# Retention and MLP on one core: first loads on other queues, another order of loads and blocks, and casts one burst later

## The chip, the core and the metric

The kernel runs on one core of a Trainium2 chip. The core has five engines with instruction streams of their own: TensorE (PE, matmuls), VectorE (DVE), ScalarE (ACT), GpSimd (POOL) and SyncE (SP). SP, ACT and POOL can issue DMA transfers. The metric is the device time of one execution, in microseconds (us); lower is better.

## The reference, cut to what matters

```python
# q, k, v: (8, 8, 576, 64) f32: batch, heads, positions, head width
scores = (1 / sqrt(64)) * q @ k.T                    # per batch and head
gamma  = 1 - 2 ** (-5 - arange(8))                   # one per head
Dmat   = where(i >= j, gamma ** (i - j), 0)          # i, j: positions
x = ((scores * Dmat) @ v) -> (4608, 512)             # tokens x (heads * width)
h = x @ w_in                                         # w_in:  (512, 2048)
g = maximum(0.01 * h, h)
out = g @ w_out                                      # w_out: (2048, 512), out f32
```

The first part is retention: attention with a decay in place of the softmax. It can be computed in chunks, with a running state per head that is carried from chunk to chunk. The second part is an MLP with a leaky activation.

## The kernel before, in words

**Units and groups.** The 4608 tokens are cut into 36 units of 128 tokens (two chunks of 64). Four units make a group of 512 tokens; there are nine groups. A batch has nine chunks, so in some units (4, 13 and so on) the second chunk begins a new batch. The three loads of such a unit are split into two DMAs each.

**What a unit goes through.** `load` brings k, q and v of the unit (256 KB each) into three buffers, six of each kind. `cast_k` (ACT, L172) turns k into f16; `cast_q` (L175) and `cast_v` (L179) multiply by a decay table and turn into f16, on DVE for units 0 to 7 and on POOL later. q and k are then transposed: on PE for units 0 to 7 (`transpose_pe`, L200, with a copy out of PSUM at L207; `turn` is both), by a DMA on SP for later ones (`transpose_dma`, L183). `scores` (L215, L224) computes q times k and each chunk's contribution to the state; `masks` (L233) applies the causal mask; `state` (L255 to L261) adds to the running state and `state_cast` (L273, L276) makes the f16 copy of it. `outputs` (L291, L302) or `outputs_acc` (L321, L333) computes the unit's x. With `outputs`, two steps bring x into the f16 tile xT: `own` (ACT, L355) and `add` (DVE, L360). With `outputs_acc` one copy does (`x_copy`, ACT, L341).

**The MLP.** The first product (`h_mm`, L373) works on blocks of w_in columns, with the leaky step behind each on ACT (L387). `h_half` takes two column blocks and 256 tokens, `h_unit` four blocks and the 128 tokens of one unit, `h_block` one block and 512 tokens. Their PSUM tiles and those of the transposes come from one pool of four. w_in is loaded in four quarters of two DMAs each by POOL, with a cast to f16; the pairs of blocks 0 and 1 of `halves` use quarter 0, 2 and 3 quarter 1, 4 and 5 quarter 2, 6 and 7 quarter 3. The second product is plain for group 0 (`wide`, L423). From group 1 on it is a scheme of seven half-size products (`seven`, L483) on sums of g (`mix`) and of w_out (`mix_weights`). In `seven` the first product is copied out by ACT (`keep`, L495, the tile k1) before PE may go on adding to the same PSUM tile.

**What sets the order.** The order on each engine is the order of the calls, written out by hand (`manual_schedule`). Each engine runs its instructions in that order, and waits where an operand isn't ready. Some names:

- `burst(u)`: scores of u, outputs of u - 1, masks, state and state cast (POOL) of u, own and add of u - 1.
- `ahead(u)`: cast of k on ACT, of q and v on POOL, and the DMA transpose on SP.
- `step(u)`, in the steady part: `burst(u)`, `load(u + 4)`, `ahead(u + 2)`.
- `early(u)`, L758: the form of `step` for units 9 to 12. `early(9)` is called in the wide products, `early(10)` between them and `seven(1, ...)`, `early(11)` and `early(12)` by hooks after the first and the fifth product of `seven(1, ...)`.
- `keep_warm(n)`: products of zeros into an unused tile.
- `settle`, `finish`, `finish2`: state and masks of a unit; its outputs and what brings them to xT.

In the first 50 us the order is a long list by hand (L560 to L756): POOL issues most loads, SP a few, and units 0 to 7 run between the blocks of groups 0 and 1.

Of the kernel before, what the change touches and what calls it, by code (L numbers as in the profile page):

```python
# [18 lines left out]
def kernel(  # L19
# [9 lines left out]
    nc = tc.nc  # L29
# [54 lines left out]
    def behind(dma, *others):  # L84
        for o in others:
            tc.add_manual_dep(
                dma.ins,
                o.ins.name,
                mybir.DependencyInfo(
                    mybir.DependencyClass.Sync, mybir.DependencyReason.DATA  # L90
                ),
                reason="order of loads",
            )
# [17 lines left out]
    last_load = {}  # L111
    carry = [None]

    def half(i):
        return slice(CH * i, CH * i + CH)
# [3 lines left out]
    def load(u, eng=None, after=None):  # L119
        for x in (1, 0, 2):  # L120
            t = ld_pool.tile([P, H, D], FP, name=f"t32_{x}")
            t32[u, x] = t
            c = 2 * u
            same = c % CB + 1 < CB
            e = eng[x] if isinstance(eng, dict) else eng or nc.sync
            engs = e if isinstance(e, tuple) else (e,)
            n = H // len(engs)
            for j, rows in ((0, P),) if same else ((0, CH), (1, CH)):
                b, w = (c + j) // CB, (c + j) % CB
                for i, e in enumerate(engs):  # L130
                    hs = slice(n * i, n * i + n)
                    d = e.dma_start(  # L132
                        out=t[CH * j : CH * j + rows, hs],
                        in_=(q, k, v)[x][b, hs, CH * w : CH * w + rows, :].rearrange(
                            "h t d -> t h d"
                        ),
                    )
                    if after is not None and (x in after or not isinstance(after, dict)):
                        behind(d, *(after[x] if isinstance(after, dict) else after))
                        after = None  # L140
                    last_load[u, x] = d
# [3 lines left out]
    def load_w_in(f, after=None):  # L145
        fs = slice(f * FQ, (f + 1) * FQ)
        rows = moe_w_in.rearrange("(o c k) f -> o k c f", o=2, k=CH)
        ds = []
        for o in range(2):
            ds.append(nc.gpsimd.dma_start(out=w_in16[half(o), :, fs], in_=rows[o][:, :, fs]))  # L150
            if after is not None and not o:
                behind(ds[0], *after)
        return ds
# [20 lines left out]
    def cast_q(u, eng):  # L174
        eng.tensor_tensor(out=qk16[u][:, 0], in0=t32[u, 0], in1=decay(u, 0), op=MUL)  # L175
# [91 lines left out]
    def live(u, j):  # L267
        return (2 * u + j) % CB != CB - 1

    def state_cast(u, copy, js=(0, 1)):  # L270
        js = [j for j in js if live(u, j)]
        if len(js) == 2:
            copy(out=st16[u], in_=s32s[u])  # L273
        else:
            for j in js:
                copy(out=st16[u][:, j], in_=s32s[u][:, j])  # L276
# [94 lines left out]
    def h_mm(hps, n, g, f, ts):  # L371
        for c in range(NP):
            nc.tensor.matmul(  # L373
                out=hps[:, n, :],
                lhsT=w_in16[:, c, f * P : (f + 1) * P],
                rhs=xT[g][:, c, ts],
                start=(c == 0),
                stop=(c == NP - 1),
            )

    def g_tile(g):
        if g not in g_t:
            g_t[g] = g_pool.tile([P, NF, TOK], F16, name="gt")
        return g_t[g]

    def leaky(out, in_):
        nc.scalar.activation(out=out, in_=in_, func=mybir.ActivationFunctionType.Lrelu)  # L387
# [13 lines left out]
    def h_unit(u, fb):  # L401
        g, t0 = u // 4, (u % 4) * P
        ts = slice(t0, t0 + P)
        hps = acc_pool.tile([P, 4, P], FP, name="acc")
        for n in range(4):
            h_mm(hps, n, g, 4 * fb + n, ts)
        leaky(g_tile(g)[:, 4 * fb : 4 * fb + 4, ts], hps)
# [140 lines left out]
    def keep_warm(n):  # L548
        t = acc_pool.tile([P, 1, TOK], FP, name="acc")
        for _ in range(n):  # L550
            nc.tensor.matmul(out=t[:, 0, :], lhsT=idle[:, 0:P], rhs=idle, start=True, stop=True)
# [6 lines left out]
    pool_copy, act_copy, dve_copy = nc.gpsimd.tensor_copy, nc.scalar.copy, nc.vector.tensor_copy  # L558

    keep_warm(7)  # L560
    load(0, {1: nc.sync, 0: (nc.sync, nc.gpsimd), 2: nc.gpsimd})
    load(1, {1: nc.sync, 0: nc.gpsimd, 2: nc.gpsimd})
    load(2, nc.gpsimd)
    load(3, {1: nc.sync, 0: nc.gpsimd, 2: nc.gpsimd}, {1: (last_load[1, 1],)})
    load_w_in(0)
    load_w_in(1)
    load_w_in(2)
    load(4, nc.gpsimd)
    load_w_in(3)
    for u in range(5, 8):  # L570
        load(u, nc.gpsimd)
    w_out_loads = [d for n in range(4) for d in load_w_out(n)]


# [10 lines left out]
    for u in range(4):  # L585
        n = u + 1
        scores(u)
        if not u:
            keep_warm(3)
        state(u, 0)  # L590
        state_cast(u, dve_copy, (0,))
        masks(u)
        if not u:
            cast_q(1, nc.vector)
            cast_v(1, nc.vector)
        state(u, 1)
        if n < 4:
            transpose_pe(n, 1)
            transposed(n, 1, act_copy)
            if not u:  # L600
                keep_warm(3)
                outputs_acc(0)
                x_copy(0)
                keep_warm(1)
            transpose_pe(n, 0)
            transposed(n, 0, act_copy)
            keep_warm(3 if u else 2)
        if n < 3:
            cast_k(n + 1)
            cast_q(n + 1, nc.vector)  # L610
            cast_v(n + 1, nc.vector)
        state_cast(u, act_copy, (1,))
        if u == 1:
            outputs_acc(1)
            x_copy(1)
            keep_warm(2)
        elif u == 2:
            outputs_acc(2)
            x_copy(2)


    def halves(g, *items):
        for a, fb in items:
            h_half(g, a, fb)

    def cast_qv(u):
        cast_q(u, nc.vector)
        cast_v(u, nc.vector)

    def turn(u, x):  # L630
        transpose_pe(u, x)
        transposed(u, x, dve_copy)
# [7 lines left out]
    def finish(u):  # L640
        outputs_acc(u)
        x_copy(u)
        state_cast(u, act_copy, (1,))

    def finish2(u):
        outputs(u)
        own(u)
        add(u)
# [6 lines left out]
    def burst(u, out=True):  # L655

        if u < NU:
            scores(u)
        if out:
            outputs(u - 1)  # L660
        if u < NU:
            masks(u)
            state(u, 0)
            state(u, 1)
            state_cast(u, pool_copy)
        if out:
            own(u - 1)
            add(u - 1)

    def ahead(u):  # L670

        if u >= NU:
            return
        cast_k(u)
        cast_q(u, nc.gpsimd)
        cast_v(u, nc.gpsimd)
        transpose_dma(u)
# [10 lines left out]

    halves(0, (0, 0), (0, 1))
    finish2(3)  # L690
    halves(0, (0, 2), (0, 3), (1, 0))
    cast_k(4)
    cast_qv(4)
    halves(0, (1, 1), (1, 2))
    turn(4, 1)
    halves(0, (1, 3))
    turn(4, 0)
    halves(0, (0, 4))
    scores(4)
    settle(4)  # L700
    halves(0, (0, 5), (1, 4))
    finish2(4)
    state_cast(4, act_copy, (1,))
    halves(0, (1, 5))
    cast_k(5)
    cast_qv(5)
    halves(0, (0, 6), (0, 7))
    turn(5, 1)
    halves(0, (1, 6))
    turn(5, 0)  # L710
    halves(0, (1, 7))
    scores(5)
    settle(5)
    cast_k(6)
    cast_qv(6)
    h_unit(4, 0)
    turn(6, 1)
    cast_k(7)
    h_unit(4, 1)
    finish(5)  # L720
    turn(6, 0)
    h_unit(5, 0)
    scores(6)
    settle(6)
    cast_qv(7)
    h_unit(5, 1)
    turn(7, 1)
    halves(1, (0, 4))
# [2 lines left out]
    halves(1, (0, 5))  # L731
    scores(7)
    settle(7)
    halves(1, (0, 6), (0, 7))
    load(8, after=(w_out_loads[2],))
    load(9)
    h_unit(6, 0)
    finish(7)
    h_unit(6, 1)
# [4 lines left out]
    mix_weights(1, 0)  # L744
    mix_weights(1, 1)
    halves(1, (1, 4))
    ahead(8)
    load(10)
    mix_weights(2, 0)
    mix_weights(2, 1)  # L750
    halves(1, (1, 5), (1, 6))
    ahead(9)
    load(11)
    mix_weights(3, 0)
    mix_weights(3, 1)
    halves(1, (1, 7))  # L756

    def early(u, out=True):  # L758
        burst(u, out)
        if 8 < u < 12:  # L760
            ahead(u + 3)
            load(u + 5)

    at = {
        0: lambda: mixes(1, 0),
# [1 line left out]
        3: lambda: mixes(1, 1),  # L767
        4: lambda: (burst(8, False), ahead(11), load(13)),
        7: lambda: mixes(1, 2),
        9: lambda: early(9),  # L770
    }
    for n in range(16):
        wide(n // 4, n % 4)
        if n in at:
            at[n]()
    early(10)
    seven(1, {0: [lambda: early(11)], 4: [lambda: early(12)]})

    first = [f for i in range(4) for f in (i, i + HF)]
    second = [f for i in range(4, 8) for f in (i, i + HF)]  # L780
# [46 lines left out]
```

## Time and profile before

| | |
|---|---|
| six runs, median | 295.99 us |
| six runs, lowest and highest | 293.57 and 296.88 us |
| the profiled execution | 296.88 us, of it 295.1 us of span |
| mean granted TensorE clock | 0.992 |
| PE busy | 284.0 us, 96% of the span |
| DVE, ACT, POOL busy | 58%, 49%, 35% |
| DMA | 50.01 MB, mean 169 GB/s |

The span is the time from the first to the last instruction of the profiled execution. Busy shares are averages over the whole span: stages with different limits lie behind them. In the lines of the timeline the first number is the start in us and the second the length. In square brackets stands how long the engine had been idle before, and what ended that wait. In tables of windows there follow, for each stretch, the busy us (and number of instructions) of PE, PE's weight loads, DVE, ACT and POOL, then the granted clock, the busy share of the DMA engines (over 1 where queues overlap) and GB/s.

### The profile page before, as it was taken

What the parts mean: (1) busy time and instruction counts of PE and PEld (TensorE: products, weight loads), DVE (VectorE), ACT (ScalarE), POOL (GpSimd) and SP (SyncE); (2) the same over time, 40 slices, a digit from 0 to 9 for tenths busy, and PEclk for the clock granted to TensorE, in tenths of its full rate; (3) what the DMA queues carried; (4) which work ended last, traced back from release to release, by engine and by line L of the source; (5) the groups of instructions that cost most, each with busy time, mean ns of one, the idle gap of its engine ahead of it and who ended that gap; (6) DMA issues with size and microseconds to landing.
All of it is one profiled execution on the core that took longest, in us unless ns stands there. A gap on an engine that the chain in (4) does not pass through costs nothing.

```text
span 295.1 us, 9446 instructions
## 1 busy us (share of the span) xinstructions
PE 284.0 (96%) x4118; PEld 193.1 (65%) x4118; DVE 170.0 (58%) x293; ACT 143.8 (49%) x254; POOL 103.7 (35%) x124
## 2 busy tenths in 40 slices
PE   7898999999699999999999999999999999999994
PEld 3567887745585478547854785478448844884583
DVE  1874478954543477357736763577358546740342
ACT  3657765623224761476157515751674166306610
POOL 8859602536340333333424342334225414000000
PEclk9999999999899999999999999999999999999999
DMA  7999999499999996986599767979995251002003
GB/s 219 274 235 202 294 197 194 105 244 177 185 235 218 285 207 156 256 191 157 131 227 223 175 142 203 217 93 179 246 216 133 50 178 38 4 37 108 0 2 142
DMA packets 132218, 50.01 MB, mean 169 GB/s; under 512 B 121776, under 2 KB 126512, under 8 KB 132176
## 3 DMA queue, kind: packets, MB, share of 16 engines
q1 hardware_dynamic: 125904, 39.73, 59.9%
q0 software_dynamic: 5984, 9.57, 14.6%
q8 instruction: 32, 0.52, 0.7%
q10 hardware_dynamic: 288, 0.11, 0.1%
q14 instruction: 10, 0.08, 0.1%
HBM read 36.81 MB, written 9.44 MB: 157 GB/s over the span
## 4 chain that ended last, share of the span: by engine, by line
PE 87%; DMA 3%; DVE 3%; POOL 2%; SPq 2%; ACT 1%; issue 1%; DVEq 0%; POOLq 0%
PE acc L373 41%; PE acc L483 34%; PE acc L423 4%; PE sc L215 3%; DMA t<-in_v_dram 2%; POOL t L132 2%; PE sc L224 1%; PE ot L291 1%; PE ot L302 1%; SPq L132 1%; DMA t<-in_q_dram 1%; PE ot L321 1%; PE acc L200 1%; DVE s L233 1%; SPq L183 1%
## 5 line engine op out<-in xcount | busy, mean ns | idle before, releaser
L373 PE MATMUL acc<-xT,w_in 128*128 128x512 f16 (+2 forms) x768 | 130.9, 326 | 1.2 <-DVE xT L360 0.8
L387 ACT ACTIVATE gt<-acc 128x512 f16<-128x512 f32 x144 | 85.8, 598 | 57.5 <-PE acc L373 55.7
L373 PEld LDWEIGHTS <-w_in 128*128 128x128 f16 x768 | 68.2, 98 | 52.7 <-issue 1.5
L483 PEld LDWEIGHTS <-gt 128*128 128x128 f16 x640 | 62.0, 98 | 11.3 <-issue 2.0
L233 DVE TENSOR_TENSOR s<-sc,cs 128x512 f16<-128x512 f32 x36 | 24.7, 686 | 41.6 <-PE sc L224 39.5
L483 PE MATMUL acc<-w_out,gt 128*128 128x256 f16 x384 | 46.3, 274 | 2.3 <-ACT k L495 2.1
L273 POOL CAST st<-s 128x512 f16<-128x512 f32 x21 | 12.8, 611 | 81.9 <-DVE s L257 53.7
L175 POOL TENSOR_TENSOR qk<-t,cs 128x512 f16<-128x512 f32 x28 | 29.9, 1069 | 31.5 <-DMA t<-in_q_dram 28.6
L355 ACT COPY own<-ot 128x512 f32<-128x512 f32 x30 | 17.6, 586 | 36.5 <-PE ot L302 29.2
L179 POOL TENSOR_TENSOR v<-t,cs 128x512 f16<-128x512 f32 x28 | 31.4, 1122 | 2.3 <-DMA t<-in_v_dram 1.4
L172 ACT CAST qk<-t 128x512 f16<-128x512 f32 x36 | 22.3, 619 | 20.2 <-DMA t<-in_k_dram 13.2
L483 PE MATMUL acc<-w_mix,mix 128*128 128x256 f16 x256 | 30.8, 280 | 0.0
L467 DVE TENSOR_TENSOR mix<-gt 128x1024 f16<-128x1024 f16 x16 | 14.1, 880 | 29.0 <-ACT gt L387 29.0
L483 PE MATMUL acc<-w_mix,gt 128*128 128x256 f16 x256 | 30.6, 273 | 0.0
L483 PEld LDWEIGHTS <-mix 128*128 128x128 f16 x256 | 25.7, 101 | 3.8 <-DVE mix L467 0.2
L360 DVE TENSOR_TENSOR xT<-ot,own 128x512 f16<-128x512 f32 x30 | 20.5, 683 | 4.6 <-ACT own L355 4.6
L257 DVE TENSOR_TENSOR s<-sc,s 128x256 f32<-128x256 f32 x40 | 16.8, 419 | 3.2 <-PE sc L224 2.7
L508 DVE TENSOR_TENSOR osb<-acc,u 128x512 f32<-128x512 f32 (+1 forms) x17 | 11.1, 656 | 8.0 <-PE acc L483 8.0
L215 PEld LDWEIGHTS <-qkT 64*64 64x64 f16 x576 | 7.7, 107 | 11.3 <-issue 10.4
L423 PE MATMUL acc<-w_out,gt 128*128 128x512 f16 x64 | 14.3, 379 | 0.0
L276 POOL CAST st<-s 128x256 f16<-128x256 f32 x7 | 3.2, 456 | 31.3 <-DVE s L261 17.3
L467 DVE TENSOR_TENSOR mix<-mix,gt 128x1024 f16<-128x1024 f16 x16 | 13.1, 827 | 0.5
(52 smaller groups left out, 240.9 us busy)
## 6 DMA issues: line engine op xcount, KB each, us to landing
out_dram<-osb SPq DMA_DIRECT2D x17, 512.0 KB, 3.7
t<-in_k_dram SPq DMA_DIRECT2D x28, 256.0 KB, 3.7
t<-in_q_dram SPq DMA_DIRECT2D x25, 256.0 KB, 4.2
t<-in_v_dram SPq DMA_DIRECT2D x25, 256.0 KB, 4.9
w_in<-in_moe_w_in_dram POOLq DMA_DIRECT2D x8, 256.0 KB, 7.9
w_out<-in_moe_w_out_dram POOLq DMA_DIRECT2D x4, 512.0 KB, 10.4
t<-in_v_dram POOLq DMA_DIRECT2D x7, 256.0 KB, 5.7
t<-in_q_dram POOLq DMA_DIRECT2D x6, 256.0 KB, 5.9
```

The costliest lines, as they stand in the source:

```text
L172: nc.scalar.copy(out=qk16[u][:, 1], in_=t32[u, 1])
L175: eng.tensor_tensor(out=qk16[u][:, 0], in0=t32[u, 0], in1=decay(u, 0), op=MUL)
L179: eng.tensor_tensor(out=v16[u], in0=t32[u, 2], in1=decay(u, 1), op=MUL)
L233: nc.vector.tensor_tensor(out=s16s[u], in0=sc_tiles[u][:, :, 0], in1=mask_sb.unsqueeze(1).unsqueeze(1).to_broadcast([P, 2, NP, CH]), op=MUL,)
L257: nc.vector.tensor_tensor(out=to, in0=st, in1=carry[0], op=ADD)
L355: nc.scalar.copy(out=owns[u], in_=ot_tiles[u][:, :, 0:NP].rearrange("q j c t -> q c j t"))
L360: nc.vector.tensor_tensor(out=x_of(u).rearrange("q (c g) t -> q c g t", g=2), in0=ot_tiles[u][:, :, NP : 2 * NP].rearrange("q g (c j) t -> ...
L373: nc.tensor.matmul(out=hps[:, n, :], lhsT=w_in16[:, c, f * P : (f + 1) * P], rhs=xT[g][:, c, ts], start=(c == 0), stop=(c == NP - 1),)
L387: nc.scalar.activation(out=out, in_=in_, func=mybir.ActivationFunctionType.Lrelu)
L423: nc.tensor.matmul(out=ys[tb], lhsT=g_t[0][:, f, tb * P : (tb + 1) * P], rhs=w_out16[:, f, :], start=(f == 0), stop=(f == NF - 1),)
L467: nc.vector.tensor_tensor(out=z[:, fs], in0=a[:, fs], in1=b[:, fs], op=op)
L483: nc.tensor.matmul(out=r[name][:, tb, :], lhsT=lhs[:, f, tb * P : (tb + 1) * P], rhs=rhs[:, f, :], start=fresh and n == 0, stop=f == HF - ...
```

## The change

- **First loads.** The second half of q of unit 0 (heads 4 to 7) is issued by ACT instead of POOL; the first half stays on SP. k of unit 3 is issued by POOL instead of SP, without the dependency on k of unit 1.
- **Order on POOL.** The loads of unit 4 are issued ahead of quarter 2 of w_in, and those of unit 5 ahead of quarter 3, where before they stood after quarter 2 and after quarter 3.
- **State cast of unit 3.** Its second part moves from before the first two half blocks to after `finish2(3)`.
- **Blocks.** In groups 0 and 1 the half blocks, the two unit blocks of unit 4, the turns and the casts of unit 7's q and v are put in another order. The number of blocks stays the same.
- **Loads 8 to 11.** Loads 8 and 9 are called ahead of two half blocks, loads 10 and 11 ahead of `ahead(8)` and `ahead(9)` instead of behind them.
- **Casts.** `ahead(13)` and `load(15)` move from after `burst(10)` to after `burst(11)`, `ahead(14)` and `load(16)` from after `burst(11)` to after `burst(12)`.

```diff
--- before.py
+++ after.py
@@ -558,17 +558,18 @@
     pool_copy, act_copy, dve_copy = nc.gpsimd.tensor_copy, nc.scalar.copy, nc.vector.tensor_copy
 
     keep_warm(7)
-    load(0, {1: nc.sync, 0: (nc.sync, nc.gpsimd), 2: nc.gpsimd})
+    load(0, {1: nc.sync, 0: (nc.sync, nc.scalar), 2: nc.gpsimd})
     load(1, {1: nc.sync, 0: nc.gpsimd, 2: nc.gpsimd})
     load(2, nc.gpsimd)
-    load(3, {1: nc.sync, 0: nc.gpsimd, 2: nc.gpsimd}, {1: (last_load[1, 1],)})
+    load(3, nc.gpsimd)
     load_w_in(0)
     load_w_in(1)
+    load(4, nc.gpsimd)
     load_w_in(2)
-    load(4, nc.gpsimd)
+    load(5, nc.gpsimd)
     load_w_in(3)
-    for u in range(5, 8):
-        load(u, nc.gpsimd)
+    load(6, nc.gpsimd)
+    load(7, nc.gpsimd)
     w_out_loads = [d for n in range(4) for d in load_w_out(n)]
 
 
@@ -609,7 +610,8 @@
             cast_k(n + 1)
             cast_q(n + 1, nc.vector)
             cast_v(n + 1, nc.vector)
-        state_cast(u, act_copy, (1,))
+        if u < 3:
+            state_cast(u, act_copy, (1,))
         if u == 1:
             outputs_acc(1)
             x_copy(1)
@@ -688,41 +690,42 @@
 
     halves(0, (0, 0), (0, 1))
     finish2(3)
+    state_cast(3, act_copy, (1,))
     halves(0, (0, 2), (0, 3), (1, 0))
     cast_k(4)
     cast_qv(4)
-    halves(0, (1, 1), (1, 2))
+    halves(0, (1, 1))
     turn(4, 1)
+    halves(0, (1, 2))
+    turn(4, 0)
     halves(0, (1, 3))
-    turn(4, 0)
-    halves(0, (0, 4))
     scores(4)
     settle(4)
-    halves(0, (0, 5), (1, 4))
+    halves(0, (0, 4), (0, 5))
     finish2(4)
     state_cast(4, act_copy, (1,))
-    halves(0, (1, 5))
     cast_k(5)
     cast_qv(5)
-    halves(0, (0, 6), (0, 7))
+    halves(0, (1, 4), (1, 5))
     turn(5, 1)
-    halves(0, (1, 6))
+    h_unit(4, 0)
     turn(5, 0)
-    halves(0, (1, 7))
+    h_unit(4, 1)
     scores(5)
     settle(5)
     cast_k(6)
     cast_qv(6)
-    h_unit(4, 0)
+    halves(0, (0, 6), (0, 7))
+    finish(5)
+    halves(0, (1, 6))
     turn(6, 1)
     cast_k(7)
-    h_unit(4, 1)
-    finish(5)
+    halves(0, (1, 7))
     turn(6, 0)
+    cast_qv(7)
     h_unit(5, 0)
     scores(6)
     settle(6)
-    cast_qv(7)
     h_unit(5, 1)
     turn(7, 1)
     halves(1, (0, 4))
@@ -731,9 +734,9 @@
     halves(1, (0, 5))
     scores(7)
     settle(7)
-    halves(1, (0, 6), (0, 7))
     load(8, after=(w_out_loads[2],))
     load(9)
+    halves(1, (0, 6), (0, 7))
     h_unit(6, 0)
     finish(7)
     h_unit(6, 1)
@@ -744,22 +747,21 @@
     mix_weights(1, 0)
     mix_weights(1, 1)
     halves(1, (1, 4))
+    load(10)
     ahead(8)
-    load(10)
     mix_weights(2, 0)
     mix_weights(2, 1)
     halves(1, (1, 5), (1, 6))
+    load(11)
     ahead(9)
-    load(11)
     mix_weights(3, 0)
     mix_weights(3, 1)
     halves(1, (1, 7))
 
-    def early(u, out=True):
-        burst(u, out)
-        if 8 < u < 12:
-            ahead(u + 3)
-            load(u + 5)
+    def early(u, n):
+        burst(u)
+        ahead(n)
+        load(n + 2)
 
     at = {
         0: lambda: mixes(1, 0),
@@ -767,14 +769,14 @@
         3: lambda: mixes(1, 1),
         4: lambda: (burst(8, False), ahead(11), load(13)),
         7: lambda: mixes(1, 2),
-        9: lambda: early(9),
+        9: lambda: early(9, 12),
     }
     for n in range(16):
         wide(n // 4, n % 4)
         if n in at:
             at[n]()
-    early(10)
-    seven(1, {0: [lambda: early(11)], 4: [lambda: early(12)]})
+    burst(10)
+    seven(1, {0: [lambda: early(11, 13)], 4: [lambda: early(12, 14)]})
 
     first = [f for i in range(4) for f in (i, i + HF)]
     second = [f for i in range(4, 8) for f in (i, i + HF)]
```

## The prediction

> **What bounds the kernel now.** I read the page's busy shares first, then the matmul engine's waits, then the chain of waits, then the timeline around each hole, and last the windows of one microsecond.
>
> The page says that the matmul engine is nearly always busy, so the end moves only by closing its holes, by raising its clock, or by letting useful matmuls start sooner.
>
> ```profile
> PE 284.0 (96%) x4118; PEld 193.1 (65%) x4118; DVE 170.0 (58%) x293; ACT 143.8 (49%) x254; POOL 103.7 (35%) x124
> ```
>
> The waits of that engine name the holes (engine, line, releaser, us in total, times, longest):
>
> ```profile
> PE acc L483 <- ACT k L495: 2.1, 1, 2.1
> ...
> PE acc L373 <- DVE xT L360: 0.8, 1, 0.8
> PE acc L200 <- DVE v L179: 0.6, 1, 0.6
> ...
> PE acc L373 <- ACT xT L341: 0.3, 1, 0.3
> ```
>
> The timeline shows the largest: the cast of unit 13's k (L172) sits on ScalarE ahead of the copy k1 (L495) and waits 3.04 us for its load; the matmul waits for the copy.
>
> ```profile
> 76.33 0.62 ACT L172 CAST qk<-t 128x512 f16<-128x512 f32 x1 [3.04 <-DMA t<-in_k_dram]
> 76.85 0.58 ACT L495 COPY k<-acc 128x512 f32<-128x512 f32 x1
> 77.48 2.34 PE L483 MATMUL acc<-w_out,gt 128*128 128x256 f16 x16 [2.06 <-ACT k L495]
> ```
>
> The chain (start, us, what) gives a second price: these 64 products take 8.81 us behind the hole, and the same 64 one group later 7.15. The windows say why: the granted clock (the figure after the five engines) is 0.50 for three microseconds.
>
> ```profile
> 77.48 8.81 PE acc L483 x64
> ...
> 108.32 7.15 PE acc L483 x64
> ```
> ```profile
> 79.00:80.00 1.00, 1.00 (x6) 0.74 (x5) 0.00 (x0) 0.00 (x0) 0.20 (x1) 0.50 1.00 363
> 80.00:81.00 1.00, 1.00 (x7) 0.71 (x5) 0.00 (x0) 0.00 (x0) 0.44 (x1) 0.50 2.60 140
> 81.00:82.00 1.00, 1.00 (x7) 0.69 (x6) 0.00 (x0) 0.00 (x0) 1.00 (x2) 0.50 0.98 57
> ```
>
> Before 24 us the engine is filled with dummy products; there the first data and VectorE set the pace. VectorE waits 4.54 us for q of unit 0, then 0.92 for v; at 23.03 it adds only after ScalarE's copy, which stood behind the state cast (1.88 idle).
>
> ```profile
> 1.27 0.94 POOL L132 DMA_DIRECT2D t<-in_q_dram  x1 [0.82 <-POOLq L811]
> 2.21 0.92 POOL L132 DMA_DIRECT2D t<-in_v_dram  x1
> 5.83 0.69 DVE L175 TENSOR_TENSOR qk<-t,cs 128x512 f16<-128x512 f32 x1 [4.54 <-DMA t<-in_q_dram]
> 7.44 0.69 DVE L179 TENSOR_TENSOR v<-t,cs 128x512 f16<-128x512 f32 x1 [0.92 <-DMA t<-in_v_dram]
> 21.13 0.41 ACT L276 CAST st<-s 128x256 f16<-128x256 f32 x1 [1.88 <-DVE s L261]
> 23.03 0.69 DVE L360 TENSOR_TENSOR xT<-ot,own 128x512 f16<-128x512 f32 x1 [1.93 <-ACT own L355]
> 23.77 2.78 PE L373 MATMUL acc<-xT,w_in 128*128 128x256 f16 x24 [0.81 <-DVE xT L360]
> ```
>
> **The base of the sum.** The profiled execution took 296.88 us: 295.1 of span and 1.8 around it. It is the slowest of six; the median, 295.99, is 0.9 lower, the lowest 3.3 lower. The sum is made against 296.88.
>
> **First unit.** GpSimd's first issue goes: every later one up to v of unit 2 comes one issue, 0.9 us, earlier. k of unit 3 moves from SP to GpSimd and takes the freed place, so q and v of unit 3 and all w_in issues keep their times. ScalarE gains one issue (0.57 us by SP's row for the same half). It falls ahead of the table load at 1.64, and the cast of k at 3.69 has 0.56 idle before it: +0.05, and k's path is not the last. When does q land? The rows of this size: 4.0 us from SP, 4.5 from GpSimd. From an issue at about 1.65 that is 5.6 to 6.1, with another ring in the contest; against that, nothing stands ahead of it on its ring but two constants. I take 5.5 against 5.77 before: -0.3; bounds -0.7 and +0.4. The Trainium skill, page "DMA: Bandwidth & Descriptors", section "Issuing engines are not separate DMA queues", says that a second issuing engine saves only the issue time, as all share the same 16 engines. The trace agrees that they are full (DMA share 1.03 and 1.14 in 2 to 4 us); by the rule q gains nothing and only v does. I stay near the row because q saves its rival: v is issued at 1.27 and lands near 6.4 instead of 7.4, so it no longer sets the second half of the scores (8.19, behind v's cast ending 8.13; the first half allows 8.05): -0.15. v of unit 2 (idle 0.21 at 12.32) is 0.9 us earlier and loses SP's k3 as a competitor: -0.2. Beyond this VectorE is busy from 9 to 18 us and hides earlier data. Sum -0.65; by the rule -0.35.
>
> **The state cast of unit 3 behind its copy.** On ScalarE the two leaky steps and the copy own (0.59) no longer wait for VectorE's 21.09. The outputs end near 20.5 after the shift, own follows at 20.7 to 21.3, the add ends at 22.0, and the next two halves keep the matmul engine until 22.3: the hole of 0.81 closes, -0.81. The cast itself (0.41) is needed only by unit 4's outputs, 8 us later: 0.
>
> **Blocks reordered.** Each half block is 0.93 us. (a) The turn of unit 4's k now has one half ahead of it instead of two. Before, the half (1,0) began at 23.77, its leaky at 24.84, the cast of k ended at 25.95: 2.18 after the start. One more half ends 1.86 after it: with the hand-over of 0.05 a new hole, +0.37. (b) Unit 5's copy to xT has the half (1,6), both turns and (1,7) behind it: hole gone, -0.34. (c) The casts of unit 7 move ahead of unit 6's scores, so the last turn no longer waits for them: -0.59. (d) The price: VectorE copies turn (6,0) until 0.31 us before scores(6), then casts twice (1.28), so unit 6's state starts 0.87 after the scores instead of 0.51; masks end at 2.68, the engine arrives at 2.47: +0.25. The distances from scores 4 and 5 to their outputs stay at 2.2 us against masks ready within 1.9: 0.
>
> **Units 4 and 5 ahead of w_in.** A GpSimd issue that waits starts just after the landing of the one eight places before it: the second k half of unit 4 at 14.74, v of unit 3 having landed at 14.45. The bytes are FIFO; w_in's second quarter still lands at 20.0 and its user comes at 20.4. Then, by the rows, six halves at 0.38 each: unit 4 from 20.4 to 22.3 (before 22.95 to 24.8), in time for casts at 22.3. The third quarter's second part is issued after 20.0 and lands near 24.8 (4.5 us as the late quarter did); the engine reaches block (0,4) near 27: 2.2 us of cover. The last quarter lands near 29.7, needed at 34: 4 us. Unit 5 lands 25.6 to 27.3, needed at 30.8. Cost 0; with cover gone, each us late is a us.
>
> **SP's queue.** Loads 10 and 11 go past the transposes of 8 and 9. Load 8 waits for w_out, expected 2 us earlier than 44.9; nine issues of about 0.9 us hold SP to 51, while the transpose of 8 waits for a cast at about 53 anyway (it sat 4.7 us at that wait): 0. All later SP work moves up: load 13 from 71.8 to about 66.5, its k landing near 71.7. Moving loads 8 and 9 past two halves crosses nothing on SP: 0.
>
> **Casts of 13 and 14 one burst later.** ScalarE's casts, GpSimd's four casts, transposes 13 and 14, and loads 15 and 16 all move. k1 is now ahead of cast 13 on ScalarE: the hole of 2.06 goes; the 0.17 for the add before it stays. Late next: transpose 13 after about 76 against burst 13 near 89, transpose 14 after 83 against burst 14 near 97: 13 us, the later groups' usual distance. On GpSimd they fall behind the state casts of 11 and 12, which therefore come earlier. 0 besides -2.06.
>
> **Clock.** The 64 products lose 8.81 - 7.15 = 1.66 us. The skill, page "TensorE: Matmul & The Clock Gate", section "HAM oscillation — how this bites in real kernels", puts the limit at idle gaps over about 3.4 us. The hole here is 2.06, so by the rule it isn't the cause and nothing comes back (sum -3.8). The row differs: the only drop in the steady part begins 1.4 us after the only large hole. I take the row: -1.66.
>
> **Sum.** -0.65 - 0.81 + 0.37 - 0.34 - 0.59 + 0.25 - 2.06 - 1.66 = -5.49; 296.88 - 5.49 = 291.4, 4.6 under the median.
>
> **Rivals.** About 0.5% is the least that a measurement of this kernel can tell from no change: 1.5 us, that is 294.5 and 297.5.
> (1) Both holes go and the clock returns: 291.4, own range 289.8 to 292.8; 0.70.
> (2) The clock drops all the same, from another hole or the rule's reading, or the front only trades waits: 291.4 + 1.7 = 293.1, either way about; for it, (a) and (d) are new holes in the front; 0.17.
> (3) Both fail: only 2.06 comes back, 294.8, no change; 0.08.
> (4) Slower: the third w_in quarter is late. The place is block (0,4) near 27. For it: its two issues wait for earlier landings and stand behind six halves. Against it: 2.2 us of cover. A stall of x costs x, plus 1.66 of clock if over 2. It decides the sign from about 5.3 us of stall, a landing after 32: 297.5 or more; 0.05.
> That the casts move but ScalarE is blocked anyway is excluded, because k1 precedes cast 13 in order.
>
> **Numbers.** Faster: (1), (2) and a little of (3): 0.87; same 0.08; slower 0.05. The range adds the profiled run's place above the median below (291.4 - 1.8) and reaches (2) and part of (3) above: 289.6 to 294.3.
>
> **What would show it.** Right: no wait of L483 on k L495; granted clock 1.0 around 75 to 83, and a piece of 64 products at 7.15; L360 no releaser of L373 near 22; VectorE's q cast near 5.5 and v directly behind; the first w_out products near 55.0 instead of 56.73; a small wait of L200 for L172 near 24. Wrong: w_in as a releaser of L373, transposes as a releaser of L215, or 0.5 in the clock elsewhere.

## The result, and the profile after

| | before | after |
|---|---|---|
| median | 294.58 us (72 runs, 292.51 to 297.55) | 293.47 us (35 runs, 290.98 to 297.32) |
| profiled execution | 296.88 us, span 295.1 | 292.40 us, span 290.6 |

The ratio of the times is 0.9946, with a 95% interval of 0.9927 to 0.9966: faster by half a per cent, where the sum had said 1.6% against the six runs shown. The four executions of the changed kernel that lie more than 1.5% above its fastest are left out of this ratio. The single times of the changed kernel do not lie around one value: 14 of 35 are between 291.0 and 292.4, and 17 between 293.2 and 294.9. The forecast, 291.4, is the lower group; the median lies at the edge of the upper one. What separates the two groups is the matter of this study. The profiled execution belongs to the lower group.

The waits of the matmul engine after the change (engine, line, releaser, us in total, times, longest):

```profile
PE acc L200 <- DVE qk L175: 1.4, 1, 1.4
...
PE acc L200 <- ACT qk L172: 0.3, 1, 0.3
...
PE acc L373 <- issue: 0.2, 1, 0.2
```

The waits for k1 (2.1), xT (0.8 and 0.3) and v's cast (0.6) are gone. A new one heads the list: the turn of q of unit 0 waits for its cast. The small one below is the hole (a) of the prediction, at 25.9 us. The timeline has both ends of the story (start, length; in brackets the idle time before and what ended it):

```profile
1.26 1.09 POOL L132 DMA_DIRECT2D t<-in_v_dram  x1 [0.82 <-POOLq L813]
1.72 0.53 ACTq L132 DMA_DIRECT2D t<-in_q_dram  x1
6.95 0.69 DVE L175 TENSOR_TENSOR qk<-t,cs 128x512 f16<-128x512 f32 x1 [5.66 <-DMA t<-in_q_dram]
7.56 0.68 DVE L179 TENSOR_TENSOR v<-t,cs 128x512 f16<-128x512 f32 x1
7.70 0.40 PE L200 MATMUL acc<-ident,qk 128*128 128x128 f16 x4 [1.41 <-DVE qk L175]
...
73.83 0.59 ACT L495 COPY k<-acc 128x512 f32<-128x512 f32 x1 [1.08 <-PE acc L483]
74.72 1.92 PE L483 MATMUL acc<-w_out,gt 128*128 128x256 f16 x16
75.38 0.62 ACT L172 CAST qk<-t 128x512 f16<-128x512 f32 x1
```

At the start, ScalarE's half of q was issued at 1.72 and landed 5.1 us later; the cast starts at 6.95 instead of 5.83. v is ready at once behind it, as expected, but that helps nothing. At 74 us the copy k1 now comes before the cast of unit 13 and the products follow without a hole. In the chain the 64 products behind it (start, us, what) cost about what they cost in later groups (7.15 before):

```profile
74.78 7.09 PE acc L483 x64
```

### The profile page after: what moved, and what is told of

Its sections match the earlier page's. It is cut to its first block, busy times and chain, and to the rows that moved or that the text cites. A ratio compares the mean times of both kernels' runs of the same rounds, so it can differ in the third digit from the quotient of the medians.

```text
span 290.6 us, 9449 instructions
## 1 busy us (share of the span) xinstructions
PE 281.8 (97%) x4118; PEld 191.8 (66%) x4118; DVE 170.4 (59%) x293; ACT 144.2 (50%) x254; POOL 105.3 (36%) x124
## 4 chain that ended last, share of the span: by engine, by line
PE 88%; DMA 4%; POOL 4%; DVE 2%; issue 1%; ACT 0%; DVEq 0%; POOLq 0%
PE acc L373 41%; PE acc L483 34%; PE acc L423 5%; POOL t L132 3%; DMA w_in<-in_moe_w_in_dram 3%; PE sc L215 3%; DMA t<-in_q_dram 1%; PE ot L291 1%; PE sc L224 1%; PE ot L302 1%; POOL w_in L150 1%; PE acc L200 1%; PE ot L321 1%; DVE s L233 0%; DVE s L261 0%
## 5 line engine op out<-in xcount | busy, mean ns | idle before, releaser
L175 POOL TENSOR_TENSOR qk<-t,cs 128x512 f16<-128x512 f32 x28 | 31.1, 1109 | 15.5 <-DMA t<-in_q_dram 15.5
L467 DVE TENSOR_TENSOR mix<-gt 128x1024 f16<-128x1024 f16 x16 | 14.8, 932 | 28.8 <-ACT gt L387 28.8
L483 PE MATMUL acc<-w_mix,mix 128*128 128x256 f16 x256 | 29.5, 273 | 0.0
L483 PEld LDWEIGHTS <-mix 128*128 128x128 f16 x256 | 25.0, 98 | 3.1 <-DVE mix L467 0.2
```

Of the source, the lines that this page charges most:

```text
L467: nc.vector.tensor_tensor(out=z[:, fs], in0=a[:, fs], in1=b[:, fs], op=op)
L483: nc.tensor.matmul(out=r[name][:, tb, :], lhsT=lhs[:, f, tb * P : (tb + 1) * P], rhs=rhs[:, f, :], start=fresh and n == 0, stop=f == HF - ...
```

## The experiments

Theory H: the late q opens a hole at the start, and in about half of the executions the matmul clock drops to half behind it; this makes the upper group. Theory E: the clock drops elsewhere, and the first loads cost only their delay. A table stands behind the experiments that brings their starts together.

**The changed kernel again.** No edit.

> The changed kernel once more, as it is. Its single times stood in groups: 14 of 35 from 291.0 to 292.4 us, 17 from 293.2 to 294.9. Both theories expect the same two groups. Theory H (the start): the late q of unit 0 opens a hole of 1.4 us on the matmul engine at 6.3 us, and in about half of the executions the clock loses a window of some 3.4 us soon after it; an execution of the upper group then shows a granted clock of 0.5 for about 3 us before 25 us. Theory E (elsewhere): the drop lies in other places, after the small holes of 24 to 26 us or in the steady part; an execution of the upper group shows it there.

Median 293.19 us (ratio to before 0.9941, 0.9916 to 0.9967), again in two groups: nine times from 291.4 to 292.4, twelve from 293.0 to 294.9. This time the profile shows an execution of the upper group (294.9, of it a span of 293.1). Its timeline and its windows (behind the stretch: busy us and instructions of PE, its weight loads, DVE, ACT and POOL, then the granted clock, DMA share and GB/s):

```profile
7.75 0.69 DVE L175 TENSOR_TENSOR qk<-t,cs 128x512 f16<-128x512 f32 x1 [6.47 <-DMA t<-in_q_dram]
8.50 0.61 PE L200 MATMUL acc<-ident,qk 128*128 128x128 f16 x4 [2.52 <-DVE qk L175]
8.90 1.49 PE L551 MATMUL acc<-idle 128*128 128x512 f16 x3
```
```profile
8.00:9.00 1.00, 0.50 (x5) 0.50 (x6) 1.00 (x2) 0.00 (x0) 1.00 (x2) 0.77 1.04 344
9.00:10.00 1.00, 1.00 (x5) 0.21 (x2) 0.04 (x1) 0.85 (x2) 1.00 (x3) 0.50 1.00 332
10.00:11.00 1.00, 1.00 (x34) 0.62 (x34) 0.00 (x0) 0.25 (x1) 1.00 (x3) 0.50 1.02 340
11.00:12.00 1.00, 1.00 (x3) 0.33 (x3) 0.95 (x3) 0.00 (x0) 1.00 (x3) 0.53 1.08 354
```

q was still later, the hole 2.52, and the clock is at 0.50 from 8.54 to 11.95. Three dummy products took 1.49 us instead of 0.81. The first useful product started at 21.47 instead of 19.29; no other place up to the last product shows a drop. This is what H said.

This is one profile, but the mean granted clock of every execution is on record. In the first set of the changed kernel (36 executions with a clock, one more than the times above), all 15 up to 292.4 have a mean of 0.997 or more, and 15 of the 17 from 293.2 to 294.9 have 0.994 or less, which is what one such drop makes of 290 us. In the second set it is nine of nine, and nine of the twelve. So most of the upper group has lost the clock once. The mean does not tell where. For the few of the group that have a full mean the cause is not shown; a late start of full speed, met below, would not appear in it.

**Old first loads.**

```diff
-    load(0, {1: nc.sync, 0: (nc.sync, nc.scalar), 2: nc.gpsimd})
+    load(0, {1: nc.sync, 0: (nc.sync, nc.gpsimd), 2: nc.gpsimd})
...
-    load(3, nc.gpsimd)
+    load(3, {1: nc.sync, 0: nc.gpsimd, 2: nc.gpsimd}, {1: (last_load[1, 1],)})
```

> The changed kernel with the first loads as before the change: second half of q of unit 0 from GpSimd, k of unit 3 from SP behind k of unit 1. Theory H: q's cast starts near 5.8 again instead of 6.95, the hole at 6.3 shrinks to 0.3, scores of unit 0 come 0.7 us earlier, the useful matmuls near 0.5 to 0.7 earlier; the lower group stands near 290.9 and holds most executions, so the median is near 291.2. Theory E: the lower group moves by the same 0.5 to 0.7, but the upper group stays as large; the median is near 292.9. If the first loads do not matter: 293.5.

Median 291.93 us, 1.3 below the changed kernel beside it (ratio to before 0.9907, 0.9868 to 0.9946). All nine times are between 291.1 and 292.6: the upper group is gone, so E falls. None of the nine has a mean clock under 0.997. The lower group did not move to 290.9; a wait appeared that the later front had covered. Its timeline:

```profile
57.71 1.74 SPq L132 DMA_DIRECT2D t<-in_v_dram  x1
59.63 3.04 SPq L183 DMA_TRANSPOSE qkT<-qk  x2
64.82 0.32 PE L215 MATMUL sc<-qkT 64*64 64x64 f16 x16 [0.63 <-DMA qkT<-qk]
```

The transpose of unit 9 stands on SP behind load 11, which the change put there, and its casts had ended at 56.0. The better version below removes this wait.

**Late casts alone,** on the kernel before: the new `early`, and the calls `early(9, 12)`, `burst(10)`, `early(11, 13)`, `early(12, 14)`.

```diff
-    early(10)
-    seven(1, {0: [lambda: early(11)], 4: [lambda: early(12)]})
+    burst(10)
+    seven(1, {0: [lambda: early(11, 13)], 4: [lambda: early(12, 14)]})
```

> The kernel before with one part of the change: casts and transposes of units 13 and 14, and loads 15 and 16, one burst later. The profile should show no wait of the second product for the copy k1 and no 0.5 in the clock at 79 to 82. Lowest of the kernel before is 292.5, so some of its executions already lack both. Expected: the group above 295.3 (20 of 72) empties, the median falls from 294.6 by 0.6 to 1.5. If the hole and its clock drop were in every execution: minus 3.7. If the part does nothing: 0.

Median 292.87 us, 1.8 below before (0.9943, 0.9923 to 0.9963). The times lay between 292.1 and 297.7 before and lie between 292.3 and 294.0 now. No wait for k1 is left and the clock stays at 1.0 up to the last product. The lowest time did not fall: the best executions of the kernel before had already been free of this loss. The mean clocks say how often the clock drop occurred: of the 62 executions of before beside this run, 20 of the 21 above 295.3 us have 0.994 or less, and none of the other 41. So the drop is in a third of them, and the median execution of before does not have it.

**New first loads alone,** on the kernel before: the reverse of the diff of the old first loads.

> The kernel before with one part of the change: second half of q of unit 0 from ScalarE's queue, k of unit 3 from GpSimd. Theory H: q's cast at 6.9 to 7.0, a hole of 1.4 us at 6.3, the first useful product 0.5 us later than 18.81, slower by 0.5 in the lower group and by 1 to 1.5 in the median (more executions with a clock drop). Theory E: slower by 0.5 in both. My recorded working had a gain of 0.65 here.

Median 296.89 us: 2.2 slower in the median, and by the ratio 1.005 (1.002 to 1.008). The prediction had a gain of 0.65 for this part. The profile's timeline shows a second way in which the late q can cost, which H had not said:

```profile
7.57 0.61 PE L200 MATMUL acc<-ident,qk 128*128 128x128 f16 x4 [1.20 <-DVE qk L175]
7.97 1.49 PE L551 MATMUL acc<-idle 128*128 128x512 f16 x3
...
11.65 1.49 PE L551 MATMUL acc<-idle 128*128 128x512 f16 x3
```

Three dummy products still take 1.49 us at 11.65; in the kernel before, three took 0.82 at 8.44. Here the engine had not come to full speed yet when the hole came. The trace's record of the clock begins where full speed is granted: at 7.12 us in the profile of before, and at 13.79 in this one. That the hole made it late is likely, not shown. The first useful product started at 21.70. The copy k1 was waited for here too, 1.6 us, with no drop behind it: the hole without the drop that the mean clocks tell of.

**q from GpSimd, k of unit 3 as changed.** The first line of the diff of the old first loads alone.

> The changed kernel with one line back: the second half of q of unit 0 from GpSimd; k of unit 3 stays on GpSimd. GpSimd then has ten issues ahead of w_in instead of nine, so w_in is issued 0.9 us later. Theory Q (the second queue for q is what costs): q's cast starts near 5.7 to 5.9, no hole over 1.3 us near 6, executions stand as with all old first loads: median 291.9, none of them over 293. Theory K (the move of k of unit 3 counts too): the first useful product moves by 0.3 us or more against 18.50, median 292.3 to 292.8. If w_in decides: it waits at the first block, near 19.3.

Median 292.54 us, six times from 291.4 to 293.0 (0.9913, 0.9887 to 0.9938). q's cast starts at 5.27, there is no hole, and the first useful product stands at 18.58 against 18.50 with all old loads. By the starts that is theory Q. The median lies where theory K had put it (292.3 to 292.8), 0.6 above that of all old loads. The two kernels ran on different chips, so that k's move costs something is neither shown nor excluded.

**The hole filled.** Only dummy products are added to the changed kernel.

```diff
     transposed(0, 1, act_copy)
-    keep_warm(3)
+    keep_warm(7)
```

> The changed kernel with seven products of zeros instead of three between the turns of k and q of unit 0. They add no useful work and end near 7.8 us at half clock, 6.4 at full clock; q still lands at 6.9 or later. Theory H (the idle hole is what costs the clock): no 0.5 in the granted clock before 25 us and no cold products after 8 us in most executions; the upper group (293.2 to 294.9) shrinks from half to a fifth or less, median near 291.8. Theory L (the late q itself costs, the clock follows the phase of the chip's own window and not the hole): two groups as before, median 293.2.

Median 291.97 us (0.9899, 0.9876 to 0.9921): six of seven times from 291.7 to 292.1, one of 293.2. q is still late; in the profile, that of the 293.2, it is later than in any other kernel, and the products behind it run at full speed all the same:

```profile
4.69 1.67 PE L551 MATMUL acc<-idle 128*128 128x512 f16 x7
8.86 0.40 PE L200 MATMUL acc<-ident,qk 128*128 128x128 f16 x4 [2.50 <-DVE qk L175]
9.09 0.81 PE L551 MATMUL acc<-idle 128*128 128x512 f16 x3
```

More work ahead of the wait, and the upper group is gone while the late load is not: it was mostly the clock, and the idle time made it. All seven mean clocks are 0.997 or more. One reserve stands: this ran on another chip than the run of the changed kernel above, which was not repeated there. But even this execution has a hole of 2.50 and no drop, so the hole's length alone does not decide.

**Holes by dose.** On the kernel with old first loads, ScalarE reads the first product's PSUM tile a few times more before k1, into a scratch tile; what is computed stays the same.

```diff
             product(name, lhs, rhs, fresh)
+            if n == 0 and 2 <= g <= 7:
+                for _ in range(g - 1):
+                    nc.scalar.copy(out=scratch, in_=r["p1"])
             then()
```

> The changed kernel with old first loads and artificial holes: in groups 2 to 7 ScalarE makes 1, 2, 3, 4, 5 and 6 needless copies of the first product ahead of the copy k1, so the matmul engine idles there for about 0.5, 1.1, 1.7, 2.3, 2.9 and 3.4 us (0.59 each less the burst of 0.67 that covers k1). Sum of the idle time about 12 us. Theory H: from about 2 us on the granted clock falls to 0.5 for some 3.4 us after the hole, 1.7 us lost each: two to four drops, 3.4 to 6.8 us more than the idle time. The skill's limit of about 3.4 us: at most the last hole is followed by a drop.

307.24 us, one run. The holes were 0.52, 1.14, 1.76, 2.37, 2.99 and 3.61 us. Behind the first four the clock stays at 1.0; behind each of the last two it is at 0.5 for 3.41 us (two of the windows behind the fifth):

```profile
228.21 2.75 PE L484 MATMUL acc<-w_out,gt 128*128 128x256 f16 x16 [2.99 <-ACT k L496]
```
```profile
230.00:231.00 1.00, 1.00 (x7) 0.67 (x6) 0.00 (x0) 0.00 (x1) 0.91 (x1) 0.50 0.02 4
231.00:232.00 1.00, 1.00 (x6) 0.71 (x5) 0.00 (x0) 0.58 (x1) 0.00 (x0) 0.50 1.03 236
```

**Six holes of one length.** The same with `range(4)` in every group.

> As the kernel with holes by dose, but four needless copies in each of the groups 2 to 7, six holes of about 2.37 us. There, holes up to 2.37 had no clock drop behind them (one try each) and those of 2.99 and 3.58 had one of about 3.6 us at 0.5; yet the kernel before lost the clock after a hole of 2.06. Theory P (the position of the hole in a window of the chip's own decides between about 2 and 3 us): one to four of the six holes are followed by a drop. Theory T (a fixed limit between 2.4 and 3.0): none of six.

311.26 us, one run. Six holes of 2.37, and a drop behind three of them (the starts of the products behind the six are 106.19, 139.12, 172.24, 203.69, 236.81 and 268.26; the drops are at 106, 140 and 205). Lines of the first, which has one, and of the third, which has none:

```profile
106.19 3.38 PE L484 MATMUL acc<-w_out,gt 128*128 128x256 f16 x16 [2.37 <-ACT k L496]
...
172.24 1.91 PE L484 MATMUL acc<-w_out,gt 128*128 128x256 f16 x16 [2.37 <-ACT k L496]
```

Equal holes, one execution, half with a drop: this is theory P. What the position is can be read from the trace's record of the clock. In each of the 14 profiles the clock changes only at points that lie whole multiples of 3.413 us apart. The three drops here start at 105.83, 139.96 and 204.82, ten and nineteen such steps apart, and each lasts one step. Where the steps fall differs between executions: full speed began at times from 3.83 to 7.12 us, and once at 13.79. The windows cut at these steps, for the first hole (103.82 to 106.19) and the third (169.87 to 172.24):

```profile
102.42:105.83 3.41, 1.40 (x71) 1.12 (x70) 3.38 (x6) 2.52 (x5) 0.36 (x1) 1.00 1.67 172
105.83:109.24 3.41, 3.05 (x15) 2.12 (x15) 2.41 (x6) 1.31 (x3) 1.30 (x2) 0.50 0.90 200
...
167.27:170.68 3.41, 2.60 (x81) 2.16 (x80) 2.50 (x4) 1.95 (x4) 0.86 (x1) 1.00 0.55 124
170.68:174.10 3.42, 1.86 (x18) 1.67 (x18) 2.68 (x6) 2.48 (x5) 1.19 (x2) 1.00 0.84 187
174.10:177.51 3.41, 3.41 (x34) 3.06 (x32) 0.69 (x1) 0.58 (x1) 1.43 (x2) 1.00 0.40 90
```

The first hole lies almost whole in one stretch and leaves the matmul engine 1.40 us of work there; the next stretch is at 0.50. The third is divided by a step and leaves 2.60 and 1.86; nothing follows. So it goes in all 14 profiles, up to the last product. There are nine drops, and the stretch ahead of each had 0.67 to 1.49 us of work; of the other stretches at full clock one had 1.41 and all the rest 1.86 or more. What counts is the work within a stretch, not the length of a hole, and since the steps and the landings fall differently in each execution, one kernel has groups of times. It fits the hole filled, too: its hole (6.36 to 8.86) is divided by a step at 7.33, with 2.19 and 1.86 us of work on the two sides. Without the four added products, 0.22 us each there, the first stretch would have had about 1.3 (an estimate from these figures).

**The kernel before once more.** No edit.

> The kernel before once more. Its single times run from 292.1 to 297.7 in three groups, and its lowest group lies 0.2 under the lowest of the kernel with late casts alone. Expected: another hole at the copy k1 than 2.06 (0 to 3 us), as k of unit 13 lands at another time, and a drop of the clock only if the hole is 2 us or more. If the hole is 2.06 again without a drop, the clock alone makes the groups.

296.40 us. The hole was there with another length, 1.76, and with a drop behind it. So below 2 us a drop can follow too, and my bound of 2 us was wrong; the hole of 1.76 in the run by dose had none:

```profile
PE acc L483 <- ACT k L495: 1.8, 1, 1.8
```
```profile
78.00:79.00 1.00, 1.00 (x7) 0.71 (x5) 0.21 (x1) 0.00 (x0) 0.95 (x1) 0.50 1.48 262
79.00:80.00 1.00, 1.00 (x7) 0.69 (x6) 0.00 (x0) 0.00 (x0) 0.65 (x2) 0.50 0.67 93
```

**All of q from SP.** The changed kernel, with `0: nc.sync` for q of unit 0.

> The changed kernel with all of q of unit 0 from SP, behind k of unit 0; v of unit 0 stays GpSimd's first issue. In the changed kernel SP's half landed at 4.35 us, ScalarE's half (issued at 1.72) at 6.86. Theory S (a third queue with its own constants ahead gets its data late): from SP both halves land by 5.3 to 5.6, no hole over 0.5 near 6, no execution over 293, median 291.6 to 292.2. Theory V (v of unit 0 asked for earlier takes the bandwidth): q lands at 6.3 or later whoever issues it, hole of 1 us or more, two groups, median near 293.

Median 291.15 us, four times from 290.9 to 291.4 (0.986, 0.9793 to 0.9928). q lands 4.5 us after its issue at 1.25 and v is ready directly behind it:

```profile
5.88 0.69 DVE L175 TENSOR_TENSOR qk<-t,cs 128x512 f16<-128x512 f32 x1 [4.60 <-DMA t<-in_q_dram]
6.49 0.68 DVE L179 TENSOR_TENSOR v<-t,cs 128x512 f16<-128x512 f32 x1
```

v of unit 0 as GpSimd's first issue is therefore not what made q late (theory V falls), and issuing twice the bytes from one queue was faster than two halves from two. A wait of 1.1 us before the turn remained, without an upper group in four runs (mean clocks of 0.998 or more).

**q ahead of the constants.** In the changed kernel ScalarE's two loads of the identity and the tables move behind its half of q.

> The changed kernel with ScalarE's three issues in another order: half of q, then the identity and the tables. If q's half was late because 106 KB of constants stood ahead of it on the same queue: it lands near 5.5, and the constants (needed at 4.4 and 5.8) near 5.0, so that the turn of k waits 0.6 and the hole near 6 is gone; median near 292.2. If it is late because three queues share the engines: it lands at 6.3 or later, two groups, median near 293.

Median 294.07 us, no faster than before (0.998, 0.9952 to 1.0007). Its lines are numbered two lower:

```profile
5.39 0.38 PE L198 MATMUL acc<-ident,qk 128*128 128x128 f16 x4 [1.06 <-DMA ident<-ret_ident]
7.25 0.69 DVE L173 TENSOR_TENSOR qk<-t,cs 128x512 f16<-128x512 f32 x1 [5.96 <-DMA cs<-ret_consts]
```

The DMA rows (KB, us from issue to landing):

```profile
t<-in_q_dram ACTq DMA_DIRECT2D x1, 128.0 KB, 3.1
t<-in_q_dram SPq DMA_DIRECT2D x1, 128.0 KB, 3.6
cs<-ret_consts ACTq DMA_DIRECT2D x1, 74.0 KB, 4.8
```

ScalarE's half of q now landed 3.1 us after its issue at 1.20, by 4.3, but the tables took its place as the last: issued at 2.29, landed near 7.1, and q's cast needs both. On that queue whatever stood last landed at about 7 in both orders, so its place behind the constants made q late. An order with the identity last was not run. The late turn cost the clock here too: two holes, of 1.06 and 1.57, left 1.19 us of work between the steps at 4.17 and 7.59, the clock is at 0.50 from 7.59 to 11.00, and 12 of the 20 executions have a mean clock of 0.994 or less.

**A better version.** The changed kernel with the old first loads, and:

```diff
-    halves(0, (0, 2), (0, 3), (1, 0))
-    cast_k(4)
+    halves(0, (0, 2), (0, 3))
+    cast_k(4)
+    halves(0, (1, 0))
...
-    load(11)
     ahead(9)
+    load(11)
```

> The changed kernel with the old first loads, the cast of k of unit 4 ahead of the half block (1,0), and load 11 behind the transpose of unit 9 as before the change. The profile of the kernel with old first loads shows two holes that these are meant to close: 0.32 for k's cast of unit 4 at 24.7, 0.63 for the transpose of unit 9 at 64.8, where SP had issued load 11 first (57 to 59.4) though the casts were ready at 56. Expected: 291.9 - 0.9 = 291.0. Rival: the loads behind the transposes come later and ScalarE waits for k of unit 12 or 13 again, 291.9 or more.

Median 290.77 us (291.0 expected), five times within 290.6 and 290.9: a ratio of 0.9861 (0.9839 to 0.9883) to before. All five are below the lowest of the changed kernel (290.98), though not run beside it. Its waits of the matmul engine, from the second row on:

```profile
PE ot L321 <- DVE s L233: 0.8, 3, 0.3
PE acc L200 <- DVE qk L175: 0.3, 1, 0.3
PE sc L215 <- ACT qkT L207: 0.2, 1, 0.2
PE ot L291 <- DVE xT L360: 0.2, 1, 0.2
```

Neither the hole of 0.3 behind k's cast of unit 4 nor that of 0.6 behind the transpose is left.

The starts side by side, from the timelines, one execution each:

| kernel | q's cast | first useful product | first plain w_out product |
|---|---|---|---|
| before | 5.83 | 18.81 | 56.73 |
| after | 6.95 | 19.29 | 56.10 |
| after again (clock drop) | 7.75 | 21.47 | 58.56 |
| new first loads alone (slow to full speed) | 6.82 | 21.70 | 58.97 |
| q ahead of constants (clock drop) | 7.25 | 20.75 | 57.16 |
| hole filled | 8.11 | 20.51 | 56.96 |
| old first loads | 5.64 | 18.50 | 54.91 |
| q from GpSimd | 5.27 | 18.58 | 55.01 |
| all of q from SP | 5.88 | 18.20 | 54.62 |
| better version | 5.79 | 18.54 | 54.46 |

Against the old first loads, q's cast is 1.3 later in the changed kernel and the first useful product 0.8; with the hole filled it is 2.5 and 2.0. So a late q alone costs some 0.5 less than it is late by. In the execution with the drop it is 2.1 and 3.0, in the one slow to full speed 1.2 and 3.2: the clock adds about 1.4 and 2.5.

## Why the prediction was right, and where not

**The two big holes: right in place, too large for the median.** In the profiled execution both came back as written: no wait for k1 (2.06), and 7.09 for the 64 products instead of 8.81 (1.72; the sum had 1.66). The choice of the row against the rule was right for this kernel. The Trainium skill's page "TensorE: Matmul & The Clock Gate", section "HAM oscillation — how this bites in real kernels", names idle gaps over about 3.4 us; here drops followed holes of 1.76, 2.06, 2.37 (three times in six), 2.52, 2.99 and 3.61, and one of 1.57 with another of 1.06 close ahead of it. But I took one execution, the slowest of six, for the rule. Late casts alone gave 1.8 in the median, not 3.7. The part that was mis-sized, by about 1.9, is the clock's 1.66: the mean clocks put the drop in 20 of 62 executions and not in the median one, which loses about what the hole alone costs. The base of the text, 295.99 for the median, was 1.4 above that of 72 runs, as four of its six stood above 295.3, against 20 of the 72.

**The first unit: wrong in sign.** The step that failed is "When does q land?": I took 5.5, between bounds of 5.1 and 6.2, and it was 6.7 to 7.6 in the three profiles with these first loads and the dummy products unchanged. The row from which I took SP's 4.0 us was that of a queue with only k ahead. I noted that on ScalarE's queue "nothing stands ahead of it but two constants" and counted that as an advantage; it was the cause. The Trainium skill's page "DMA: Bandwidth & Descriptors", section "Issuing engines are not separate DMA queues", had warned that a second issuer buys only issue time, and even that was too kind here: q landed about 1 us later than before (6.82 against 5.80). The term was -0.65; it measured +0.48 in the profiled execution (18.81 to 19.29) and +2.2 in the median by itself, with k's move in it. The larger part of that is not the lateness but what I did not price: the new idle time at the start, at a place where the clock can still be lost. That is rival (2), to which I gave 0.17 and which holds for about half of the executions (17 of 36 by their mean clocks); I had looked for its hole at 24 us, not at 6.

**The blocks: right in the sum.** From the first useful product to the half block (1, (0, 6)) before took 28.10 us (18.81 to 46.91), after 26.99 (19.29 to 46.28): -1.11, against -0.81 + 0.37 - 0.34 - 0.59 + 0.25 = -1.12. The waits list shows the hole (a) at 0.3 (0.37 forecast). The masks' wait (d) is not in it: unit 6's outputs start 1.11 behind the start of the block ahead of them (42.70 to 43.81), 0.14 more than before and not 0.25. An idle time of 0.22 before the half block at 24.31, which the sum did not have and whose cause the profile does not tell, comes on top. So the agreement to 0.01 is chance; the parts agree to about 0.2.

**SP's queue: 0 only because the front was late.** With the front early, the transpose of 9 behind load 11 costs 0.63. The working looked at the transpose of 8 and gave no cover in microseconds for that of 9.

**w_in: right.** w_in releases no matmul in any profile; only GpSimd waits for it.

**The sum.** For the profiled execution: +0.48 - 1.11 - 2.06 - 1.72 = -4.4, against 4.5 measured (296.88 to 292.40) and 5.49 forecast. In the medians of the single parts: 294.6 - 1.8 (casts) + 2.2 (first loads) - 1.1 (blocks, from the profiles) = 293.9, against 293.2 and 293.5 measured. That 291.4 missed the median by only 2.1 is luck in part: the base, 296.88, lay 2.3 above the median of before, and the gain, 5.49, was 4.4 above the 1.1 measured; the two errors run against each other. The stated range held the result since it was drawn to take in rival (2).

## What to carry to other kernels

Before taking a stall from one profile as the gain, look at the single times: if they stand in groups, the profile shows one member, and a median gains only the share of executions that have the stall. When a first load is moved to another queue, count the bytes that stand ahead of it there, and ask what the engines that wait for it will do meanwhile: an idle matmul engine at the start can cost its clock besides the wait. Here dummy products in front of the wait, or an earlier load, were worth more than the order of what follows. And do not judge a hole by its length alone: two short ones close together cost the clock here, and a longer one that a step divided did not.

## What the runs showed of the hardware that was not expected

- Equal idle holes of 2.37 us in one execution were followed by a granted clock of 0.5 three times in six, and of two holes of 1.76 one was. In all 14 profiles the clock changed only at steps of 3.413 us, and each drop up to the last product lasted one step. The stretch before a drop had 0.67 to 1.49 us of matmul work; stretches with 1.86 or more had no drop behind them. The one of 1.41 without a drop leaves the limit somewhere from 1.4 to 1.9, as the ends of matmuls are modelled. How much work it takes to come to full speed at the start was not measured.
- The trace has no record of the clock until full speed is granted, and the windows then read 1.00: in the changed kernel's profile three dummy products take 1.48 us at 4.80 and 0.81 at 7.93, with full speed from 6.15. In the kernel with the new first loads alone this lasted to 13.79, with no figure under 1.00 in that column.
- The same 128 KB half of q landed 3.1 us after its issue as the first on ScalarE's queue and 5.1 us as the third, behind 106 KB of constants; SP's half of the same size took 3.6 and 3.1 us in the same two profiles.
